# Folded spectra for six batches, a gate spread over two quarters, and a last block finished tile by tile

## The chip, the cores and the metric

The kernel is one program on one core of a Trainium2 chip. TensorE multiplies, VectorE, ScalarE and GpSimd work on vectors, and SyncE issues the DMAs; the five run side by side and meet at semaphores. The metric is the device time of one execution in microseconds; less is better. Three runs of the kernel before took 1412.92 to 1415.26 us.

## The reference

Three layers follow each other. The first is an attention with landmarks, on 8 batches of 8 heads, 576 tokens and 64 features:

```python
A = sm(q, k_lm); Bm = sm(q_lm, k_lm); C = sm(q_lm, k)     # 32 landmarks: means over 18 tokens
Z = Bm.T / (norm1(Bm) * norminf(Bm) + 1e-6)
for _ in range(6): Z = 2 * Z - Z @ Bm @ Z
x = A @ Z @ C @ v                                          # heads side by side: [8, 576, 512]
```

The second mixes tokens and features by a Fourier transform and has a network with 2048 hidden features:

```python
u = x + real(fft(fft(x, axis=1), axis=2))
y = u + relu(layernorm(u) @ w_ch1) @ w_ch2
```

The third is a gated network with 1024 hidden features, on y and on y shifted by one token:

```python
k = relu((mu_k * y + (1 - mu_k) * y_prev) @ w_k)
out = sigmoid((mu_r * y + (1 - mu_r) * y_prev) @ w_r) * (k * k @ w_v)
```

## The kernel before, in words

The work comes in two units. A batch (`phase1`, eight of them, 0 to 7) does the attention and the Fourier transform of its 576 tokens. A block is 512 tokens; there are 9, 0 to 8. Each block goes through the second layer's network (class `Block`) and later through the third layer (class `Gated`).

A planner orders everything. Each operation of each engine is recorded with a cost and with what it depends on; then the planner places the operations one after the other, on each engine the ready one with the highest key. A key is the length of work behind the operation plus a lead, and `LEADS` holds an added lead for each part of a batch or of the weights' conversion. So one list of numbers decides the order on all five engines. TensorE's products of the blocks are a chain in a fixed order; the products of the batches are woven between them. A batch takes a PSUM bank from those that the blocks don't hold.

In a batch, `chain_a` makes the scores A against the landmarks. Tokens s and 576 − s stand beside each other (`A[c][:, 0]` and `[:, 1]`), in three tiles of 96 or 97 rows. Their sums and differences (`Ae`, `Ao`) are rounded to two f16 halves. The spectra over tokens are products of these with a cosine and a sine table of 289 columns: for each of two groups g and each table, three tiles times three pairs of halves (`PARTS`), nine products into one bank. `keep` rounds a spectrum to two f16 halves again, by a ScalarE copy and a VectorE operation. Behind that, `chain_a` transposes A itself (`AT`). `tail` uses spectra and transposes to make the batch's rows of u.

A block of the second layer has four quarters. In blocks 2 to 8 each quarter is made of seven smaller products of sums of operands (`Block.first`); the operands 0 to 6 of a block (`un`) are f16 halves, and in `run(ps, w, b, ...)` the number b names the operand: 0, 4, 5, 6, 3, 2, 1 in this order. Between the seven stand the steps of the quarter before (`second`).

A block of the gated network has two quarters (`Gated.first`, g 0 and 1), n = 2i + g in all. Beside the quarter's seven products of `w_k`, `fillers(n)` puts the steps of the quarter before (`second`) and, in the first quarter of each block, the seven products of the gate (`gate`). The gate's products share one PSUM bank: each adds to, or starts anew in, the bank that ScalarE or VectorE has just read. For n = 0 there is no quarter before. For n = 18 only the last quarter's steps are left, and the last step of each pair of output tiles is followed by a VectorE operation on each tile and a store of 256 KB.

The cosine and sine tables lie in constant memory for the whole first phase.

Of the kernel before, what the change touches and what calls it, by code (L numbers as in the profile page):

```python
# [23 lines left out]
M = 32  # L24
DM = H * D
# [6 lines left out]
HS = S // 2 + 1  # L32
WS = 64.0
# [104 lines left out]
class Op:  # L138
# [14 lines left out]
    ("back", 0): 427,  # L153
    ("back", 1): 2988,
    ("back", 2): -34,
    ("back", 3): -54,
    ("back", 4): 45,
    ("back", 5): -35,
    ("back", 7): -119,
    ("items", 0): 50,  # L160
    ("keys", 0): 61,
    ("keys", 1): -243,
    ("keys", 2): 1030,
    ("keys", 3): 261,
    ("keys", 4): -206,
    ("keys", 5): -130,
    ("keys", 6): -9,
    ("keys", 7): -191,
    ("land", 0): 509,
    ("land", 1): -1287,  # L170
    ("land", 2): -1291,
    ("land", 3): -771,
    ("land", 4): -488,
    ("land", 5): -427,
    ("land", 7): -18,
    ("norm", 0): 29,
    ("norm", 1): 2257,
    ("norm", 2): -59,
    ("norm", 5): 13,
    ("norm", 7): 148,  # L180
    ("own", 0): -2,
    ("own", 1): 169,
    ("own", 3): -3,
    ("own", 5): 809,
    ("own", 6): -23,
    ("own", 7): 51,
    ("prep", 0): 214,
    ("prep", 1): -163,
    ("prep", 2): -253,
    ("queries", 1): 141,  # L190
    ("queries", 2): 16,
    ("queries", 3): 11,
    ("queries", 4): 4,
    ("queries", 5): 57,
    ("queries", 7): -23,
    ("scales", 0): -5,
    ("series", 0): 343,
    ("series", 1): 447,
    ("series", 2): -156,
    ("series", 3): -89,  # L200
    ("series", 4): -108,
    ("series", 5): -66,
    ("series", 6): 1,
    ("series", 7): 63,
    ("sums", 1): 114,
    ("sums", 2): -77,
    ("sums", 3): -392,
    ("w1", 0): 3,
    ("w1", 1): -655,
    ("w1", 2): 258,  # L210
    ("w1", 3): 59,
    ("w2", 0): 8,
    ("w2", 1): -454,
    ("w2", 2): -64,
    ("w2", 3): 149,
# [55 lines left out]
class Plan:  # L271
# [455 lines left out]
def phase1(a, iss, psum, const, pool, ident, ublock, ones):  # L727
# [21 lines left out]
    def load_q(b):  # L749
        q = T["q", b] = tile([128, 4, 2 * HS], "q")  # L750
# [30 lines left out]
    def landmarks(b):  # L781
# [21 lines left out]
        step = 2 if b else 1  # L803
        for h in range(0, 4, step):
            sl = slice(h, h + step)
            for o, c in ((0, 0), (16, 290)):
                v_.tensor_reduce(
                    qs[:, sl, o:o + 16],
                    q[:, sl, c:c + 288].rearrange("p c (g t) -> p c g t", t=18),
                    axis=AX.X, op=ALU.add,  # L810
                )
# [3 lines left out]
    def chain_a(b):  # L815


        q, kbd = T["q", b], T["kbd", b]
        A = [
            tile([128, 512], f"A{c}")[0:97].rearrange("p (x m) -> p x m", x=2) for c in range(3)  # L820
        ]

        if b:

            ST = tile([128, 4 * HS], "ST", "s2").rearrange("p (a g s) -> p a g s", a=2, g=2)
            for ab in range(2):
                ph = psum(2)
                for p in range(4):
                    for g in range(2):
                        r = slice(64 * g, 64 * g + 64)  # L830
                        mm(
                            ph[g][M * p:M * p + M, 0:HS], kbd[r, p, g],
                            q[r, p, HS * ab:HS * ab + HS],
                            True, True, beside=2, tile_position=(64 * g, M * p),
                        )
                for g in range(2):
                    s_.activation(ST[:, ab, g], ph[g][:, 0:HS], AF.Copy)

        def scores(c):
            ps = psum()[0]  # L840
            if b:
                for ab in range(2):
                    for g in range(2):
                        o = 256 * ab + 128 * g
                        tr(ps[0:97, o:o + 128], ST[:, ab, g, 96 * c:96 * c + 97], ident)
            else:
                ps4 = ps.rearrange("p (a g h m) -> p a g h m", a=2, g=2, m=M)
                for ab in range(2):
                    o = HS * ab + 96 * c
                    for p in range(4):  # L850
                        mm(ps4[0:97, ab, :, p], q[:, p, o:o + 97], kbd[:, p], True, True)
            p3 = ps[0:97, :].rearrange("p (g m) -> p g m", m=M)
            mx = tile([97, 16], "mx", bufs=2)
# [3 lines left out]
                e, p3, mx.unsqueeze(2).to_broadcast([97, 16, M]), op=ALU.subtract  # L857
# [3 lines left out]
        def normalize(c):  # L861
            e = A[c].rearrange("p a (h m) -> p (a h) m", m=M)
            sm = tile([97, 16], "sm", bufs=2)
# [4 lines left out]
                e, e, sm.unsqueeze(2).to_broadcast([97, 16, M]), op=ALU.mult  # L868
# [3 lines left out]
        for c in range(3):  # L872
# [4 lines left out]
            iss.tile(pool, [128, 2, 768], F16, n).rearrange("p x (c m) -> p x c m", c=3)[0:97]  # L877
            for n in ("Ae", "Ao")
        ]
        for c in range(3):  # L880
            for x, op, n in ((Ae, ALU.add, "d1"), (Ao, ALU.subtract, "d2")):
                d = tile([128, HS], n)[0:97, 0:256]
# [4 lines left out]
        acs = tile([128, 4 * HS], "acs", "s2")  # L887
# [21 lines left out]
        def keep(dst, g, ps, scale, pair_scale):  # L909
            n = wide(ps)  # L910
            if b < HALF:
                s_.activation(dst[:, g, 0:n], ps, AF.Copy, scale=scale)
                return
            hi, lo = dst[:, 0, g, 0:n], dst[:, 1, g, 0:n]
# [4 lines left out]

        for g in range(2):  # L920
# [1285 lines left out]
```

## Time and profile before

| | |
|---|---|
| time, median of 3 runs | 1413.22 us (1412.92 to 1415.26) |
| the profiled execution | 1416.67 us, its span 1414.9 us |
| TensorE busy, matmuls | 1398.1 us (99%) |
| VectorE busy | 1003.2 us (71%) |
| ScalarE busy | 799.0 us (56%) |
| GpSimd busy | 462.7 us (33%) |
| mean granted clock of TensorE | 0.996 |
| DMA | 213.05 MB, mean 151 GB/s |

Times in the rows below are from the start of the span. A busy TensorE is not TensorE at its peak: matmuls overlap, and the time of one in a group is longer than the distance from its start to the next one's. PE is TensorE, DVE is VectorE, ACT is ScalarE, POOL is GpSimd, and PEld is the weight load that goes before each matmul. In a name such as `gp<-c_cosT,Ae` the output stands left of the arrow and the inputs right of it, without buffer numbers.

### The profile page before, as it was taken

The page shows a single profiled execution, that of the slowest core. Times are in us where ns is not written, and L with a number is a line of the kernel's source. Part 1 is how long each engine was busy: PE and PEld are TensorE (multiplying, and loading weights), DVE is VectorE, ACT ScalarE, POOL GpSimd, SP SyncE. Part 2 cuts the span into 40 slices and gives each one's busy share as a digit, 9 for nine tenths or more (in the row PEclk, how much of TensorE's full clock was granted, in tenths as well). Part 3 has the DMA queues.
Part 4 walks back from the last instruction along what each step waited for, and adds up shares of the span by engine and source line. Part 5 has one row for each costly group of instructions (what it writes and reads, how often), then busy time and mean ns, then how long its engine had stood idle before and what let it go on. Part 6 is the DMA issues. An engine that isn't in the chain of part 4 may idle for free.

```text
span 1414.9 us, 26712 instructions
## 1 busy us (share of the span) xinstructions
PE 1398.1 (99%) x10575; PEld 909.6 (64%) x10575; DVE 1003.2 (71%) x1934; ACT 799.0 (56%) x1579; POOL 462.7 (33%) x546
## 2 busy tenths in 40 slices
PE   8999999999999999999999999999999999999998
PEld 5555454566676666666666666666667767776775
DVE  7988874776886876886867785327778776876532
ACT  4876543454545545545565453226887767867552
POOL 3013254343252251253322270103545533652400
PEclk9999999999999999999999999999999999999999
DMA  9795763673664564654477553423110011010001
GB/s 340 262 343 177 243 240 104 211 265 121 224 205 134 201 225 138 203 186 135 151 238 289 228 194 121 157 110 120 31 61 31 31 61 61 23 38 31 31 1 60
DMA packets 86780, 213.05 MB, mean 151 GB/s; under 512 B 7168, under 2 KB 28416, under 8 KB 80384
## 3 DMA queue, kind: packets, MB, share of 16 engines
q1 hardware_dynamic: 86656, 211.36, 43.2%
q8 instruction: 83, 1.36, 0.4%
q14 instruction: 41, 0.34, 0.1%
HBM read 168.08 MB, written 43.25 MB: 149 GB/s over the span
## 4 chain that ended last, share of the span: by engine, by line
PE 90%; DVE 3%; DMA 3%; POOL 1%; ACT 1%; issue 1%; SPq 0%; DVEq 0%; ACTq 0%
PE acc L420 37%; PE ph L420 33%; PE gp L420 16%; PE gp L437 2%; DVE xt L264 2%; DMA dw<-wboth 1%; PE spare L1371 1%; DMA wst<-in_w_v 1%; DMA v<-in_v 1%; DMA wst<-in_w_ch 1%; POOL xr L264 1%; SPq L405 0%; DVE k L264 0%; POOL tmp L264 0%; DVE rm L264 0%
## 5 line engine op out<-in xcount | busy, mean ns | idle before, releaser
L420 PEld LDWEIGHTS <-w 128*128 128x128 f16 x4464 | 430.2, 98 | 268.5 <-issue 30.4
L420 PE MATMUL acc<-h,w 128*128 128x512 f16 x1728 | 429.4, 379 | 0.0
L420 PE MATMUL ph<-un,w 128*128 128x256 f16 (+1 forms) x2736 | 394.4, 288 | 1.5 <-DVE un L264 1.4
L420 PE MATMUL acc<-w_v,k 128*128 128x512 f16 x864 | 204.3, 379 | 0.0
L264 DVE TENSOR_TENSOR rm<-ph,rm 128x512 f32<-128x512 f32 x138 | 95.0, 688 | 136.4 <-ACT rm L264 97.8
L264 ACT ACTIVATE rm<-ph 128x512 f32<-128x512 f32 x156 | 93.1, 597 | 174.2 <-PE ph L420 173.8
L420 PE MATMUL ph<-xk,w_k 128*128 128x256 f16 x1512 | 180.1, 273 | 0.0
L420 PEld LDWEIGHTS <-w_k 128*128 128x128 f16 x1512 | 147.7, 98 | 27.0
L420 PEld LDWEIGHTS <-k 128*128 128x128 f16 x864 | 84.5, 98 | 78.7
L264 POOL TENSOR_TENSOR xk<-xt,xk 128x512 f16<-128x512 f32 x63 | 89.9, 1440 | 135.0 <-ACT xk L264 131.8
L264 POOL TENSOR_TENSOR xr<-xt,xr 128x512 f16<-128x512 f32 x63 | 90.8, 1455 | 21.5 <-ACT xr L264 21.5
L420 PE MATMUL gp<-w_r,xr 128*128 128x256 f16 x756 | 93.0, 273 | 3.2 <-DVE gm L264 2.1
L264 ACT ACTIVATE rm<-rm 128x512 f32<-128x512 f32 (+1 forms) x134 | 84.3, 630 | 12.6 <-DVE rm L264 9.5
L420 PEld LDWEIGHTS <-xr 128*128 128x128 f16 x756 | 73.9, 98 | 24.3 <-issue 4.0
L264 ACT ACTIVATE h<-rm 128x512 f16<-128x512 f32 x84 | 52.7, 627 | 62.1 <-DVE rm L264 61.6
L264 DVE SCALAR_TENSOR_TENSOR k<-rm,k 128x512 f16<-128x512 f32 x72 | 56.0, 781 | 25.2 <-ACT k L264 25.2
L264 DVE SCALAR_TENSOR_TENSOR h<-rm,h 128x512 f16<-128x512 f32 x84 | 63.3, 757 | 11.6 <-ACT h L264 11.3
L264 DVE TENSOR_TENSOR xt<-xt 128x512 f32<-128x512 f32 x52 | 70.4, 1373 | 1.5 <-POOL xr L264 1.1
L264 POOL TENSOR_TENSOR A<-A,sm 97x512 f32<-97x512 f32 x24 | 27.8, 1157 | 117.7 <-DVE sm L264 93.8
L264 ACT ACTIVATE h<-ph 128x512 f16<-128x512 f32 x60 | 35.7, 595 | 49.9 <-PE ph L420 49.5
L264 DVE SCALAR_TENSOR_TENSOR h<-ph,h 128x512 f16<-128x512 f32 x60 | 41.3, 688 | 28.1 <-ACT h L264 27.9
L264 DVE SCALAR_TENSOR_TENSOR xt<-yb,mus,xt 128x512 f32<-128x512 f32 x72 | 54.7, 809 | 6.9 <-POOL xt L264 6.9
(222 smaller groups left out, 2041.2 us busy)
## 6 DMA issues: line engine op xcount, KB each, us to landing
w<-dw SPq DMA_DIRECT2D x60, 1024.0 KB, 7.2
w<-dwp SPq DMA_DIRECT2D x56, 384.0 KB, 5.7
ys<-ub SPq DMA_DIRECT2D x36, 256.0 KB, 7.4
out<-sg SPq DMA_DIRECT2D x36, 256.0 KB, 2.1
yb<-ys SPq DMA_DIRECT2D x8, 1026.0 KB, 5.3
v<-in_v SPq DMA_DIRECT2D x8, 1024.0 KB, 8.2
wst<-in_w_ch SPq DMA_DIRECT2D x16, 512.0 KB, 6.5
q<-in_q SPq DMA_DIRECT2D x14, 578.0 KB, 4.9
```

Source lines behind the costliest of these rows:

```text
L264: f(real(out), *map(real, args), **{k: real(x) for k, x in kw.items()})
L420: self.nc.tensor.matmul(out.real(), lhsT=lhsT.real(), rhs=rhs.real(), start=start, stop=stop, **kw)
L437: self.nc.tensor.transpose(out.real(), in_.real(), ident.real())
L1371: nc.tensor.matmul(into.real() if into else spare[0], lhsT=z.to_broadcast([128, 128]), rhs=z.to_broadcast([128, 512]), start=not into, sto ...
```

## The change

The spectra of batches 2 to 7 are folded once more. The tokens 0 to 288 are ordered in three runs, `RUNS`: 0 to 90, the odd ones from 91, the even ones from 90. The columns of q are laid out in that order by the host for these batches. The output frequencies s and 288 − s share the sums over even tokens and, up to a sign, the sums over odd tokens. So `folded` makes two sums of 145 columns each, over even and over odd tokens, four groups of three products in all, in one bank. ScalarE copies the odd sums out, VectorE writes sum and difference as one spectrum of 289 columns, and `keep` rounds that as before. The tables `cosP` and `sinP` are new. Batches 0 and 1 keep the old way, and their tables are now one load into a place that the operands 4, 5 and 6 of blocks 2 to 8 use later. The transposes `AT` write their columns of PSUM with a step of two for two of the three runs.

In the gated network the last two products of block 0's gate move from its first to its second quarter. At the end, the last quarter's steps go tile by tile, and the last of the four tiles is multiplied and stored in two halves of columns.

The planner's cost of a transpose depends on its width now, and `LEADS` is another list throughout; three of its lines stand here for all.

```diff
+QS = S // 4 + 1
+RUNS = (range(0, 91), range(91, 288, 2), range(90, 289, 2))
+TS = 290
...
-    ("back", 0): 427,
-    ("back", 1): 2988,
-    ("back", 2): -34,
...
+    ("back", 0): 808,
+    ("back", 1): 3753,
+    ("back", 2): 292,
...
-        self.record("pe", run, 0.108, [out], [in_, ident])
+        self.record("pe", run, wide(ident) / 1200.0 + 0.003, [out], [in_, ident])
...
-    cosT = load_const("cosT", [128, 2, 3, HS], F16)
-    sinT = load_const("sinT", [128, 2, 3, HS], F16)
+    cosT, sinT = [early[:, n] for n in range(2)]
+    iss.load(early, a["early"])
     cs = load_const("cs", [128, 4, 512])
+    iss.lead = 0.0
+    cosP = load_const("cosP", [128, 2, 4, QS], F16)
+    sinP = load_const("sinP", [128, 2, 4, QS], F16)
+    iss.lead = was
...
+        else:
+            for h in range(4):
+                for o, c, n in ((0, 0, 0), (16, TS + 1, 1)):
+                    v_.tensor_reduce(
+                        qs[:, h, o:o + 5], q[:, h, c:c + 90].rearrange("p (g t) -> p g t", t=18),
+                        axis=AX.X, op=ALU.add,
+                    )
+                    c += 91 - 2 * n
+                    v_.tensor_reduce(
+                        qs[:, h, o + 5:o + 16],
+                        q[:, h, c:c + 198 + 2 * n].rearrange("p (x n) -> p x n", x=2)[
+                            :, :, n:99 + n
+                        ].rearrange("p x (g t) -> p g x t", t=9),
+                        axis=AX.XY, op=ALU.add,
+                    )
...
+        RP, AT0, w = (97, (0, 96, 192), HS) if b < HALF else (100, (0, 91, 190), TS)
...
+        def spectrum(g, src, tab, dst):
+
+            ps = psum()[0]
+            for c in range(3):
+                r = 97 if c == 2 else 96
+                for n, (x, y) in enumerate(PARTS):
+                    mm(
+                        ps[:, 0:HS], src[0:r, x, c, 128 * g:128 * g + 128],
+                        tab[0:r, y, c, :], c == 0 and n == 0, c == 2 and n == 2,
+                    )
+            keep(dst, g, ps[:, 0:HS], 1.0 / SA, 1.0 / SC)
+
+        def folded(g, src, tab, dst, sign):
+
+            ps = psum()[0]
+            for x, parts in enumerate((((0, 0), (2, 3)), ((0, 1), (1, 2)))):
+                o = QS * x
+                for k, (c, n) in enumerate(parts):
+                    r = len(RUNS[c])
+                    for m, (i, j) in enumerate(PARTS):
+                        mm(
+                            ps[:, o:o + QS], src[0:r, i, c, 128 * g:128 * g + 128],
+                            tab[0:r, j, n, :], k == 0 and m == 0, k == 1 and m == 2,
+                        )
+            even, odd = ps[:, 0:QS], tile([128, QS], "odd")
+            full = tile([128, HS], "full")
+            s_.activation(odd, ps[:, QS:2 * QS], AF.Copy, scale=1.0 / SA)
+            v_.scalar_tensor_tensor(
+                full[:, 0:QS], even, 1.0 / SA, odd, op0=ALU.mult, op1=ALU.add
+            )
+            v_.scalar_tensor_tensor(
+                full[:, HS - 1:QS - 1:-1], even[:, 0:QS - 1], sign / SA, odd[:, 0:QS - 1],
+                op0=ALU.mult, op1=ALU.subtract if sign > 0 else ALU.add,
+            )
+            keep(dst, g, full, 1.0, SA / SC)
...
+            if b < HALF:
+                spectrum(g, Ae, cosT, AC)
+                spectrum(g, Ao, sinT, AS)
+            else:
+                folded(g, Ae, cosP, AC, 1.0)
+                folded(g, Ao, sinP, AS, -1.0)
...
+        runs = (RUNS[0][:-1], *RUNS[1:])
+        if b < HALF:
+            runs = [range(96 * c, 96 * c + (97 if c == 2 else 96)) for c in range(3)]
         for ab in range(2):
             for g in range(2):
                 ps = psum()[0]
-                n = HS if ab == 0 else 288
-                for c in range(3):
-                    r = 97 if c == 2 and ab == 0 else 96
+                for c, run in enumerate(runs):
+                    n = len(run)
                     tr(
-                        ps[:, 96 * c:96 * c + r], A[c][0:r, ab, 128 * g:128 * g + 128],
-                        ident[0:r, 0:r],
+                        ps[:, run[0]:run[-1] + 1:run.step], A[c][0:n, ab, 128 * g:128 * g + 128],
+                        ident[0:n, 0:n],
                     )
-                keep(AT[ab], g, ps[:, 0:n], 1.0 / SA, 1.0)
+                keep(AT[ab], g, ps[:, 0:HS], 1.0 / SA, 1.0)
...
+        early = iss.place(pa, [128, 2, 2, 3, HS], F16, "early", "more_un")
+        batch = phase1(a, iss, gp, p1c, p1w, ident, ublock, ones, early)
...
+            more = iss.spot(pa, [128, 3, 2, 2, HB], F16, "un", "more_un")
 
             def split(at, t):
-                un[at] = hi, lo = [
+                un[at] = hi, lo = [more[:, at - 4, x] for x in range(2)] if at > 3 else [
                     iss.tile(pa, [128, 2, HB], F16, "un", f"un{x}{at}") for x in "hl"
...
-                if not closes:
-                    return
+                if closes:
+                    self.store(js)
+
+            def last(self, j):
+                iss.lead = NOW
+                sl = slice(128 * j, 128 * j + 128)
+                for f in self.order[4:]:
+                    for n, (x, y) in enumerate(PARTS):
+                        mm(
+                            self.acc[j], self.ks[f // 4][:, x, f % 4, sl],
+                            ws[f"w_v{f // 4}"][:, y, f % 4], False,
+                            f == self.order[-1] and n == 2, chain=True,
+                        )
+                self.store((j,), 2 if j == 3 else 1)
+
+            def store(self, js, parts=1):
+                w = DM // parts
                 for j in js:
                     o = self.sg[j]
-                    v_.scalar_tensor_tensor(
-                        o, self.acc[j], self.qi[:, j:j + 1], self.sg[j],
-                        op0=ALU.mult, op1=ALU.mult,
-                    )
                     r0 = BLK * self.i + 128 * j
-                    iss.load(a["out"][r0:r0 + 128, :], o)
+                    for c in range(0, DM, w):
+                        v_.scalar_tensor_tensor(
+                            o[:, c:c + w], self.acc[j][:, c:c + w], self.qi[:, j:j + 1],
+                            o[:, c:c + w], op0=ALU.mult, op1=ALU.mult,
+                        )
+                        iss.load(a["out"][r0:r0 + 128, c:c + w], o[:, c:c + w])
...
-                return [late]
+                return [[partial(blocks[u].last, j) for j in range(4)]]
             if g:
-                return [late[0:1], late[1:3], late[3:5], late[5:6], late[6:7], late[7:8]]
+                full = [late[0:1], late[1:3], late[3:5], late[5:6], late[6:7], late[7:8]]
+                for k, x in enumerate(held):
+                    full[2 * k].append(x)
+                held.clear()
+                return full
...
+            if n == 0:
+                held.extend(gates[5:])
+                return [[x] for x in gates[:5]]
```

## Rows read from the trace of the kernel before

**Rows 1.** The page: busy time of each engine, share of the span, instructions.

```profile
PE 1398.1 (99%) x10575; PEld 909.6 (64%) x10575; DVE 1003.2 (71%) x1934; ACT 799.0 (56%) x1579; POOL 462.7 (33%) x546
```

**Rows 2.** Busy time of each engine in six stretches, granted clock, DMA share, GB/s.

```profile
0.00:75.00 75.00, 69.81 (x589) 42.93 (x589) 62.69 (x165) 50.57 (x119) 13.57 (x28) 0.93 0.84 293
75.00:850.00 775.00, 770.37 (x6034) 480.71 (x6023) 591.32 (x1306) 405.78 (x860) 272.92 (x339) 1.00 0.59 202
850.00:970.00 120.00, 120.00 (x794) 77.17 (x792) 46.08 (x79) 35.19 (x58) 6.03 (x14) 1.00 0.37 132
970.00:1010.00 40.00, 37.01 (x301) 28.87 (x300) 31.40 (x46) 33.99 (x61) 23.05 (x23) 1.00 0.15 54
1010.00:1395.00 385.00, 384.79 (x2795) 272.07 (x2793) 265.71 (x333) 268.54 (x476) 147.16 (x142) 1.00 0.11 39
1395.00:1414.90 19.90, 16.08 (x83) 7.82 (x81) 6.04 (x9) 4.92 (x8) 0.00 (x0) 1.00 0.15 54
```

**Rows 3.** Timeline of TensorE, two spectra of batch 5: start, length, instruction, count.

```profile
504.51 2.40 PE L420 MATMUL gp<-c_cosT,Ae 96*128 96x289 f16 x18
506.75 0.38 PE L420 MATMUL acc<-h,w 128*128 128x512 f16 x1
```

**Rows 4.** Timeline of TensorE, first quarter of the gated network; brackets: idle before, releaser.

```profile
974.93 0.39 PE L420 MATMUL gp<-eye,r 128*128 128x128 bf16 x4
...
987.09 1.47 PE L420 MATMUL gp<-w_r,xr 128*128 128x256 f16 x12 [0.70 <-ACT sg L264]
...
989.35 1.47 PE L420 MATMUL gp<-w_r,xr 128*128 128x256 f16 x12 [0.78 <-DVE gm L264]
991.95 1.47 PE L420 MATMUL gp<-w_r,xr 128*128 128x256 f16 x12 [1.13 <-DVE gm L264]
993.25 2.78 PE L420 MATMUL ph<-xk,w_k 128*128 128x256 f16 x24
```

**Rows 5.** Groups of instructions by shape, TensorE: busy us, mean ns of one, idle.

```profile
L420 PE MATMUL ph<-xk,w_k 128*128 128x256 f16 x1512 | 180.1, 273 | 0.0
L420 PEld LDWEIGHTS <-w_k 128*128 128x128 f16 x1512 | 147.7, 98 | 27.0
...
L437 PE MATMUL gp<-ident,A 96*128 96x96 f32 x80 | 10.7, 246 | 0.0
...
L420 PE MATMUL gp<-eye,r 128*128 128x128 bf16 x36 | 4.1, 219 | 0.0
```

**Rows 6.** The same view, roundings of the spectra on VectorE and ScalarE.

```profile
L264 DVE SCALAR_TENSOR_TENSOR acs<-gp,acs 128x289 f16<-128x289 f32 x24 | 10.3, 454 | 15.8 <-ACT acs L264 15.8
...
L264 ACT ACTIVATE acs<-gp 128x289 f16<-128x289 f32 x24 | 9.2, 412 | 22.5 <-PE gp L420 22.4
```

**Rows 7.** Timelines of VectorE and TensorE where block 7 is made ready.

```profile
773.85 1.28 DVE L264 SCALAR_TENSOR_TENSOR uc<-uc,gp 128x512 f32<-128x512 f32 x2
...
780.96 2.78 PE L420 MATMUL ph<-un,w 128*128 128x256 f16 x24
```

**Rows 8.** Timeline of TensorE, third product of a last quarter, next block's first two.

```profile
870.71 1.47 PE L420 MATMUL ph<-un,w 128*128 128x256 f16 x12
...
882.42 2.78 PE L420 MATMUL ph<-un,w 128*128 128x256 f16 x24
```

**Rows 9.** The first table's instructions: count, ns, first and last start in us.

```profile
L420 PE MATMUL gp<-c_cosT,Ae x144: 284/287/290, 34.2 to 715.6; 96*128 96x289 f16 x96, 97*128 97x289 f16 x48
L405 SPq DMA_DIRECT2D c_cosT<-in_cosT x1: 328/328/328, 10.7 to 10.7; - x1
```

**Rows 10.** Timeline of the end, and the page's row of the output stores.

```profile
1397.96 13.11 PE L420 MATMUL acc<-w_v,k 128*128 128x512 f16 x60
...
1400.87 0.69 DVE L264 SCALAR_TENSOR_TENSOR k<-rm,k 128x512 f16<-128x512 f32 x1 [1.42 <-ACT k L264]
1409.17 2.73 DVE L264 SCALAR_TENSOR_TENSOR sg<-acc,qi,sg 128x512 f32<-128x512 f32 x4 [7.60 <-PE acc L420]
...
out<-sg SPq DMA_DIRECT2D x36, 256.0 KB, 2.1
```

More of the change, by code (lines that the diff above doesn't have):

```diff
@@ L174 @@
[L174 to L215, printed above, removed]
+    ("back", 0): 808,
+    ("back", 1): 3753,
@@ new lines @@
+    ("back", 2): 292,
+    ("back", 3): 2,
+    ("back", 4): 804,
+    ("back", 5): 255,
+    ("back", 6): 170,
+    ("back", 7): 349,
+    ("keys", 1): -347,
+    ("keys", 2): 842,
+    ("keys", 3): -200,
+    ("keys", 4): -24,
+    ("keys", 5): -20,
+    ("keys", 6): 10,
+    ("keys", 7): 107,
+    ("land", 0): -297,
+    ("land", 1): -653,
+    ("land", 2): -89,
+    ("land", 3): -333,
+    ("land", 4): -544,
+    ("land", 5): -74,
+    ("land", 6): -180,
+    ("land", 7): -185,
+    ("norm", 0): 138,
@@ new lines @@
+    ("norm", 1): 3084,
+    ("norm", 3): -30,
+    ("norm", 4): 102,
+    ("norm", 6): 511,
+    ("norm", 7): -99,
+    ("norm", 8): -30,
+    ("own", 1): 500,
+    ("own", 2): 23,
+    ("own", 3): -84,
+    ("own", 4): 146,
+    ("own", 5): 150,
+    ("own", 6): -6,
+    ("own", 7): 404,
+    ("pairs", 0): -315,
+    ("prep", 1): 70,
+    ("prep", 2): 140,
+    ("queries", 1): 90,
+    ("queries", 2): 148,
+    ("queries", 3): 85,
+    ("queries", 4): -18,
+    ("queries", 5): 301,
+    ("queries", 6): 622,
@@ L216 @@
+    ("queries", 7): 11,
+    ("series", 1): 1044,
+    ("series", 2): -102,
+    ("series", 3): -103,
+    ("series", 4): -41,
+    ("series", 5): -137,
+    ("series", 6): -95,
+    ("sums", 0): 7,
+    ("sums", 1): -85,
+    ("sums", 2): 30,
+    ("sums", 3): 448,
+    ("w1", 1): -468,
+    ("w1", 2): 34,
+    ("w1", 3): 376,
+    ("w2", 0): 5,
+    ("w2", 1): -312,
+    ("w2", 3): 246,
 }
@@ L749, in load_q @@
     def load_q(b):
-        q = T["q", b] = tile([128, 4, 2 * HS], "q")
+        q = T["q", b] = tile([128, 4, 2 * TS], "q")
         step = 2 if b else 1
@@ L802, in landmarks @@
         qs = tile([128, 4, M], "qs")
[L803 to L810, printed above, removed]
-                )
+        if b < HALF:
+            step = 2 if b else 1
+            for h in range(0, 4, step):
+                sl = slice(h, h + step)
+                for o, c in ((0, 0), (16, 290)):
+                    v_.tensor_reduce(
+                        qs[:, sl, o:o + 16],
+                        q[:, sl, c:c + 288].rearrange("p c (g t) -> p c g t", t=18),
+                        axis=AX.X, op=ALU.add,
[5 more added lines that the diff above has]
+                        qs[:, h, o:o + 5], q[:, h, c:c + 90].rearrange("p (g t) -> p g t", t=18),
+                        axis=AX.X, op=ALU.add,
+                    )
+                    c += 91 - 2 * n
+                    v_.tensor_reduce(
+                        qs[:, h, o + 5:o + 16],
[4 more added lines that the diff above has]
+                    )
         qbd = T["qbd", b] = tile([128, 4, 2, M], "qbd")
@@ L886, in chain_a @@
         at = tile([128, 1280], "at", "s1")
-        acs = tile([128, 4 * HS], "acs", "s2")
+        acs = tile([128, 4 * TS], "acs", "s2")
         def halves(x):
@@ L2144, in consts @@
             sinT[r, c] = np.sin(ang) if s not in (0, 288) else 0.0
+    cosP = np.zeros((128, 4, QS))
+    sinP = np.zeros((128, 4, QS))
+    sp = np.arange(QS)
+    for c, run in enumerate((RUNS[0][:-1], *RUNS[1:])):
+        for r, s in enumerate(run):
+            ang = 2 * np.pi * ((s * sp) % S) / S
+            w = 0.5 if s in (0, 288) else 1.0
+            n = s % 2 if c == 0 else c + 1 if c == 1 else 3
+            cosP[r, n] = w * np.cos(ang)
+            sinP[r, n] = np.sin(ang) if s not in (0, 288) else 0.0
     cs = np.zeros((128, 4, 512))
@@ L2161, in layout @@
     qa = q[:, HPOS].reshape(B, 2, 4, S, D).transpose(0, 2, 1, 4, 3).reshape(B, 4, 128, S)
-    cols = list(range(HS)) + [0] + [S - j for j in range(1, HS)]
-    qh = np.ascontiguousarray(qa[..., cols])
+    fold = [s for run in RUNS for s in run]
+    cols = np.array([
+        [*range(HS), 0, *(S - j for j in range(1, HS)), 0, 0],
+        [*fold, *((S - s) % S for s in fold)],
+    ])[[0] * HALF + [1] * (B - HALF)]
+    qh = np.ascontiguousarray(np.take_along_axis(qa, cols[:, None, None, :], axis=-1))
     kh = np.ascontiguousarray(
```

76 lines of the change are left out of this document (24 added, 52 removed).

## The prediction

> **What bounds the kernel now.** I read the busy row of the page first: TensorE is busy 99% of the span, and no other engine is above 71% [rows 1]. A busy TensorE can still be a waiting one, so the stretches come next. From 75 to 850 us, where batches 2 to 7 are woven into the blocks of the first network, TensorE is without work for 4.6 of 775 us; from 850 to 970 us for nothing; from 1010 to 1395 us for 0.2. Three stretches leave it idle: the start (75 − 69.8 = 5.2 us), the passage into the gated network from 970 to 1010 us (3.0 us) and the end (3.8 us) [rows 2]. VectorE is at 591 of 775 us in the long stretch and ScalarE at 406. So three rules follow. Work taken off TensorE between 75 and 970 us shortens the run one for one, as long as the rest keeps up. Work put on VectorE or ScalarE there costs nothing while it is not late. A wait counts only in the three stretches named. The timelines then give the prices.
>
> **Part 1, folded spectra (batches 2 to 7).** Removed: 4 spectra of 9 products over 289 columns in each of 6 batches. In the timeline 18 of them begin at 504.51 and the next work at 506.75 us, so one takes 2.24 / 18 = 124 ns [rows 3]; 36 x 124 ns = 4.48 us a batch, 26.9 us in all. Added: 4 spectra of 12 products over 145 columns, 48 a batch. The trace of before has no full-width product of 145 columns, so I put it between neighbours. Four products of 128 columns, each with its own 128 x 128 weights, take 0.39 us from first start to last end, and one lasts 219 ns: (390 − 219) / 3 = 57 ns [rows 4, 5]. Twenty-four of 256 columns take 2.78 us, one lasts 273 ns: (2780 − 273) / 23 = 109 ns [rows 4, 5]. That is 0.41 ns a column, so 145 columns cost 57 + 17 x 0.41 = 64 ns; 48 x 64 ns = 3.07 us a batch, 18.4 us in all. The difference is 26.9 − 18.4 = 8.5 us, all of it inside the stretch in which TensorE has no slack.
>
> The bound on the other side is the weight load. A load of 128 f16 columns is shown with 98 ns [rows 5]. If loads could not overlap each other, 48 pairs would take 4.70 us against 4.48 and part 1 would cost 0.2 us a batch. I take 64 ns, because the four pairs at 57 ns each carry such a load and are the nearest row in width.
>
> Here a rule speaks against the change. The Trainium skill, page "TensorE: Matmul & The Clock Gate", section "Back-to-back issue gap", says that a stream of weight load and product pairs sustains about 81 ns at 128 columns and 131 ns at 512. By these, as an estimate, 145 columns would cost 83 ns and 289 columns 102 ns, and part 1 would add 0.3 us a batch instead of taking 1.4. The trace disagrees at both widths that it shows, 57 ns at 128 and 124 ns at 289 [rows 3 to 5], so I go by the trace.
>
> Each folded spectrum also adds a ScalarE copy of 145 columns and two VectorE operations of 145 and 144. For 289 columns these engines need 412 and 454 ns [rows 6], so at most 0.41 + 2 x 0.45 = 1.3 us a spectrum, 5.2 us a batch, and at least half of that, since the width is halved. VectorE takes on at most 24 x 0.9 = 22 us beside its 591 of 775, ScalarE 10 beside 406. The sixteen shorter sums over the queries in place of four make VectorE's share a little larger still. The cover is TensorE's own chain of blocks, which fills every gap while a batch is at VectorE. What is late next is the batch: batch 7's normalization writes its last operand source at 773.85 + 1.28 = 775.1 us, and the buffer it wants next is released by the first 12 products that start at 780.96, at 782.3 us [rows 7]. So 7.1 us of lateness are free, against at most 5.2. Cost zero.
>
> The transposes behind the spectra now write every second column of PSUM, eight of twelve a batch. No row shows such a write. One of them is shown with 10.7 / 80 = 134 ns at most [rows 5]; none extra if stride is free, and 8 x 6 x 134 ns = 6.4 us if it doubles them. I take zero, since the columns per transpose, 90 to 100 for 96 and 97, are the same, and keep 6.4 for the range.
>
> The old tables and three of the seven operand pairs now share a place. Operand 4 of the next block can no longer be written when its own buffer is free but only after the third product of the last quarter, which starts at 870.71 and ends near 872.0; it is first needed by the second product from 882.42, at 883.7 [rows 8]. Splitting it takes one operation on ScalarE and one on VectorE, so 11.7 us hold some 1.5. Cost zero. The first user of the place, block 2, comes after batch 1 is through with the tables.
>
> At the start the two tables come as one load of twice the size. The first of them was issued at 10.7 us and first used at 34.2 [rows 9], so 23 us stand for what is now one load. The folded tables, 0.6 MB more, are issued at a lower priority. Cost zero.
>
> **Part 2, gate over two quarters.** In the first quarter of the gated network nothing is left over to put between the gate's seven products, which all use one PSUM bank and so wait for its eviction. The waits stand at 987.09 (0.70 us), 989.35 (0.78) and 991.95 us (1.13) [rows 4]. The sixth and seventh product move into the second quarter, each behind products of the next stage. Those two waits, 1.9 us, go. The fifth product's wait of 0.70 stays: its release, the sigmoid, is not moved. TensorE then comes to the second quarter 1.9 + 2.6 us sooner, and what it asks for there, squares of the first quarter, must be ready. The half that is made last is wanted after 60 products of 256 columns and 24 of 512, by 0.109 us [rows 4] and 13.11 / 60 = 0.22 us [rows 10] each some 11.8 us, so I count no new wait. Gain 1.9 us; nothing if the eviction chain only makes the next product wait instead.
>
> **Part 3, the end.** Tile by tile, the last tile's products end when the last products ended before: 60 products stay 60 [rows 10]. Their inputs are wanted earlier: after 12 + 6 products of 0.22 us from 1397.96, at 1401.9 us, and they are ready at 1400.87 + 0.69 = 1401.6. That is close but no wait. Behind the last product stood one VectorE operation, 2.73 / 4 = 0.68 us, and a store that takes 2.1 us to land [rows 10]. Two halves need between 0.68 and 1.36 us, and the last store is half as large, so it may save up to 1.05 us or cost 0.68; halves overlap in part, and I take zero.
>
> **Sum.** −8.5 − 1.9 + 0 = −10.4 us. The profiled execution took 1416.67 us, of which the span is 1414.9; it becomes 1406.3, with a span of 1404.5. The median of the runs shown is 1413.22, 3.4 below it; the same subtraction gives **1402.8 us**, 0.7% faster. A difference under 0.2%, 2.8 us, is no change here.
>
> The list of priorities is new too, so every engine's order changes. What it can win is the idle time left, 4.6 us up to 850 and part of 5.2 at the start [rows 2], where the granted clock is 0.93 on average; what it can lose I set equal, 5 us.
>
> **Rivals.**
> The weights bind: 145-column products cost a weight load's 98 ns. Then part 1 costs 1.3 us, part 2 gives 1.9, and the time is 1412.6, no change. For it: the page's rule above. Against it: 57 ns pairs. Chance 0.05.
>
> The order loses what the columns gave: 3 to 8 us of new idle time, or strided transposes at 6.4: 1406 to 1411. For it: the start waits on loads and evictions, and any new order moves them. Chance 0.15.
>
> The order wins: idle time of 4 to 7 us goes as well: 1396 to 1399. For it: the idle exists; against it, it is in pieces. Chance 0.13.
>
> The batches come late (the other side): a spectrum is now a chain of product, copy, two combinations and the old pair of roundings, with one buffer each for the odd half and the whole. If a batch is late by more than the 7.1 us above, TensorE's chain of blocks stops at each of six block starts. It decides beyond 7.1 + (10.4 + 2.8) / 6 = 9.3 us; with twice my 5.2, 10.4 us, it is 6 x 3.3 − 10.4 = +9.4, and 1422.6 us. Against it: that takes twice the upper bound. Chance 0.06.
>
> No effect, because the batches already hide in time that something else sets: speaks against it that TensorE has no idle time there. 1413. Chance 0.03.
>
> **How the numbers follow.** The forecast with its own range, 1399 to 1406, has 0.58. Faster by over 0.2%: 0.58 + 0.13 + most of 0.15 = 0.84. Same: 0.05 + 0.03 and the rest, 0.09. Slower: 0.06 and a little more, 0.07. The range for 8 in 10 runs from the order that wins to the order that loses, 1396 to 1411.
>
> **What would show it.** Products of 145 columns start 64 ns apart, 288 of them (98 would refute part 1). TensorE's idle time from 75 us to the last block stays under 6 us. The second half of the gate shows no wait on its eviction. The last store starts about as long after the last product as before. Wrong it would be through waits before a block's first products, or a start that ends later than before.

## The result and the profile after

The changed kernel takes 1403.51 us (median of 6 runs, 1401.71 to 1403.63) beside 1415.16 us for the kernel before (median of 6, 1412.92 to 1415.3): ratio 0.9918, interval 0.9905 to 0.9931, 11.7 us less. The forecast was 10.4 us less and 1402.8 us. The profiled execution took 1403.63 us with a span of 1401.8. The span before was 1414.9, so the two traces differ by 13.1 us, more than the medians: the profiled execution before, 1416.67 us, was longer than each of the six runs beside it. The six runs of the changed kernel lie at 1401.7 and at 1403.5 us, with mean granted clocks of 0.998 and of 0.997 to 0.998, and what parts the two groups is not shown.

The stretches of the changed kernel, cut where its own stages end: busy time of each engine, granted clock, DMA share, GB/s.

```profile
0.00:75.00 75.00, 70.24 (x558) 41.34 (x559) 61.91 (x165) 50.22 (x118) 13.50 (x28) 0.95 0.85 298
75.00:850.00 775.00, 773.10 (x6209) 486.36 (x6203) 591.72 (x1412) 398.47 (x860) 255.93 (x317) 1.00 0.58 200
850.00:960.00 110.00, 110.00 (x728) 70.59 (x727) 66.52 (x96) 52.25 (x87) 26.37 (x38) 1.00 0.46 165
960.00:1000.00 40.00, 38.32 (x309) 29.57 (x307) 30.95 (x48) 33.75 (x61) 21.51 (x20) 1.00 0.13 46
1000.00:1382.00 382.00, 382.00 (x2781) 270.74 (x2780) 261.47 (x330) 268.23 (x474) 139.00 (x144) 1.00 0.11 40
1382.00:1401.80 19.80, 15.51 (x78) 7.45 (x76) 6.43 (x10) 4.38 (x7) 0.00 (x0) 1.00 0.15 54
```

Read beside [rows 2], TensorE is without work for 1.9 us instead of 4.6 from 75 to 850 us, and for 1.7 instead of 3.0 in the passage to the gated network; start and end change little (4.8 and 4.3 us, 5.2 and 3.8 before). VectorE is at 592 of 775 us in the long stretch, the same as before; over the whole run it grew from 1003.2 [rows 1] to 1019.0 us.

Folded products in the timeline of TensorE, one spectrum of batch 2:

```profile
201.13 0.93 PE L423 MATMUL gp<-c_sinP,Ao 91*128 91x145 f16 x12
201.90 0.60 PE L423 MATMUL acc<-h,w 128*128 128x512 f16 x2
```

Twelve of 145 columns take 0.77 us to the next work, 64 ns each, against 124 [rows 3]; one is shown with 226 ns, and (930 − 226) / 11 is 64 as well.

The passage to the gated network, the same view (brackets: idle before, releaser):

```profile
959.41 2.78 PE L423 MATMUL ph<-xk,w_k 128*128 128x256 f16 x24
...
968.00 1.47 PE L423 MATMUL gp<-w_r,xr 128*128 128x256 f16 x12 [0.34 <-ACT gm L267]
...
976.12 1.47 PE L423 MATMUL gp<-w_r,xr 128*128 128x256 f16 x12 [1.34 <-ACT sg L267]
977.43 2.78 PE L423 MATMUL ph<-xk,w_k 128*128 128x256 f16 x24
...
981.35 1.47 PE L423 MATMUL gp<-w_r,xr 128*128 128x256 f16 x12
```

The first quarter now ends with the fifth gate product at 976.12, and the second quarter begins at 977.43. The waits of 0.78 and 1.13 us ahead of the sixth and seventh product [rows 4] are gone; the sixth and the seventh run in the second quarter, at 981.35 and 990.46, with no wait. The fifth product's wait has grown from 0.70 to 1.34 us.

The end, TensorE and VectorE, and the landing of the last stores:

```profile
1384.39 13.11 PE L423 MATMUL acc<-w_v,k 128*128 128x512 f16 x60
...
1387.30 0.69 DVE L267 SCALAR_TENSOR_TENSOR k<-rm,k 128x512 f16<-128x512 f32 x1 [1.42 <-ACT k L267]
...
1394.95 0.75 DVE L267 SCALAR_TENSOR_TENSOR sg<-acc,qi,sg 128x512 f32<-128x512 f32 x1 [1.84 <-PE acc L423]
1397.55 0.88 DVE L267 SCALAR_TENSOR_TENSOR sg<-acc,qi,sg 128x256 f32<-128x256 f32 x2 [1.84 <-PE acc L423]
```

```profile
DMA to landing us min/median/max: 1.7/2.0/2.2
```

As in [rows 10], 60 products close the run, in 13.11 us. Each tile but the last is evicted while the next is multiplied. The inputs made last are ready at 1387.99, before their use. A store of half the size lands after 1.7 us instead of 2.0.

Five marks of the two traces divide the 13.1 us. The first product of block 0 starts at 66.7 us (66.2 before), +0.5. From there to the first product of the gated network it takes 892.7 us (904.8), −12.1; no_fold below, with the products of the kernel before in the same order up to there, takes 904.2, so 0.6 us of this differ between executions. The first quarter takes 18.0 us, 20.6 with the two products that left it (22.2), −1.6. From the second quarter to the last 60 products it takes 407.0 us, 404.3 without the two that came (404.7), −0.4. From there to the end of the span it takes 17.4 us (16.9), +0.5.

### The profile page after: what moved, and what is told of

It reads as the page before. It is cut to its first block, busy times and chain, and to the rows that moved or that the text cites. A ratio compares the mean times of both kernels' runs of the same rounds, so it can differ in the third digit from the quotient of the medians.

```text
span 1401.8 us, 26994 instructions
## 1 busy us (share of the span) xinstructions
PE 1389.2 (99%) x10648; PEld 906.1 (65%) x10648; DVE 1019.0 (73%) x2055; ACT 807.3 (58%) x1603; POOL 456.3 (33%) x546
## 4 chain that ended last, share of the span: by engine, by line
PE 97%; DVE 1%; ACT 1%; issue 0%; POOL 0%; DVEq 0%; ACTq 0%; POOLq 0%
PE acc L423 40%; PE ph L423 36%; PE gp L423 18%; PE gp L440 3%; PE spare L1429 1%; DVE xt L267 1%; DVE bdY L267 0%; ACT Y L267 0%; DVE uc L267 0%; DVE ub L267 0%; ACT rm L267 0%; POOL Ae L267 0%; ACT L267 0%; ACT Ae L267 0%; ACT xk L267 0%
## 5 line engine op out<-in xcount | busy, mean ns | idle before, releaser
L267 POOL TENSOR_TENSOR xr<-xt,xr 128x512 f16<-128x512 f32 x63 | 84.2, 1358 | 91.2 <-DVE gm L267 50.6
L267 POOL TENSOR_TENSOR xk<-xt,xk 128x512 f16<-128x512 f32 x63 | 86.9, 1397 | 60.6 <-ACT xk L267 60.1
L267 DVE SCALAR_TENSOR_TENSOR xt<-yb,mus,xt 128x512 f32<-128x512 f32 x72 | 60.9, 882 | 23.0 <-POOL xt L267 21.7
L267 DVE SCALAR_TENSOR_TENSOR k<-rm,k 128x512 f16<-128x512 f32 x72 | 58.0, 810 | 22.9 <-ACT k L267 22.8
L267 DVE TENSOR_TENSOR xt<-xt 128x512 f32<-128x512 f32 x52 | 64.3, 1244 | 6.9 <-POOL xk L267 4.2
L267 POOL TENSOR_TENSOR A<-A,sm 100x512 f32<-100x512 f32 (+1 forms) x24 | 26.9, 1122 | 93.4 <-DVE sm L267 79.9
L267 POOL TENSOR_TENSOR sq<-sq 128x512 f32<-128x512 f32 x18 | 23.9, 1327 | 96.1 <-ACT sq L267 96.1
```

What stands on the lines that cost most here:

```text
L267: f(real(out), *map(real, args), **{k: real(x) for k, x in kw.items()})
```

## The experiments

Each changes the changed kernel or the kernel before in one place. Ratios are to the kernel before, run on the same chip beside it; the changed kernel's own is 0.9918 (0.9905 to 0.9931).

| run | median us | ratio, interval |
|---|---|---|
| wide | 1409.96 | 0.9962 (0.9948 to 0.9975) |
| no_gate | 1407.19 | 0.9939 (0.9927 to 0.9952) |
| no_last | 1402.12 | 0.9907 (0.9892 to 0.9921) |
| old_leads | 1409.07 | 0.9952 (0.9938 to 0.9967) |
| no_fold | 1414.02 | 0.9990 (0.9981 to 0.9999) |
| new_leads | 1436.18 | 1.0152 (1.0138 to 1.0166) |
| combine_twice | 1410.38 | 0.9974 (0.9965 to 0.9983) |
| held_three | 1403.24 | 0.9917 (0.9904 to 0.9931) |
| old_list_no_zeros | 1411.47 | 0.9978 (0.9969 to 0.9986) |
| new_list_no_zeros | 1434.05 | 1.0144 (1.0127 to 1.0161) |
| combine_planned | 1404.87 | 0.9930 (0.9918 to 0.9941) |
| shaken_a | 1418.68 | 1.0030 (1.0019 to 1.0041) |

### Are the columns what counts?

**wide.** The table is padded and read past its part; the planner is told 145 columns, so the order stays.

```diff
-                            ps[:, o:o + QS], src[0:r, i, c, 128 * g:128 * g + 128],
-                            tab[0:r, j, n, :], k == 0 and m == 0, k == 1 and m == 2,
+                            ps[:, o:o + 218], src[0:r, i, c, 128 * g:128 * g + 128],
+                            tab[0:r, at:at + 218], k == 0 and m == 0, k == 1 and m == 2,
+                            planned=QS,
```

> The changed kernel in the same order on every engine, but each of the 288 folded products has 218 columns instead of 145 (the 73 more are never used). Theory A, the columns set the time: 288 x 73 columns at 0.41 ns are 8.7 us more than the changed kernel, 1412.2 us, and no new idle time of TensorE. Theory B, the gain comes from the new order and the columns are hidden: at most 2 us more. Theory C, a product costs at least its weight load's 98 ns: 218 columns cost 93 ns by columns and 98 by the load, the same price as before, so nothing is added.

```profile
L425 PE MATMUL gp<-c_cosP,Ae x144: 254/256/260, 195.2 to 720.8; 91*128 91x218 f16 x72, 100*128 100x218 f16 x36, 99*128 99x218 f16 x36
```

```profile
75.00:850.00 775.00, 773.01 (x6145) 489.20 (x6134) 586.84 (x1403) 393.06 (x853) 256.09 (x317) 1.00 0.58 199
```

The ratio rises by 0.0044, 6.2 us. The two profiled executions, which start block 0 at 66.6 and 66.7 us, differ by 1410.1 − 1401.8 = 8.3 us, close to theory A's 8.7. TensorE is without work for 2.0 us from 75 to 850 us, as in the changed kernel (1.9). Both traces have the same products in the same order. Compared start by start, 7.9 of the 8.5 us that this one loses up to the gated network lie between one folded product and the next. Theories B and C fall: the columns are not hidden, and 145 columns do not already cost a weight load's 98 ns.

**no_fold.** The kernel before with the new `fillers`, `last` and `store`.

```diff
+            if n == 0:
+                held.extend(gates[5:])
+                return [[x] for x in gates[:5]]
...
-                return [late]
+                return [[partial(blocks[u].last, j) for j in range(4)]]
```

> The kernel before with only the gate over two quarters and the last block tile by tile; spectra, tables and priorities as before. Theory A, the columns made most of the gain: 1.5 to 2.5 us faster than before, ratio 0.9985. Theory B: the spectra were hidden, so the gain is the gate's and the end's and the order's; also about 2 us, but then the list alone must bring 9 us.

It is 0.0010 faster than before, 1.4 us (0.1 to 2.7), a little under theory A's range. So parts 2 and 3 without part 1 bring about a tenth of the gain. Theory B expects nearly the same time here; what speaks against it is that the list alone does not bring 9 us (new_leads below). In the trace, the way from the gated network's first product to that of its second block takes 39.5 us, against 41.8 in the kernel before.

### The gate and the end

**no_gate.**

```diff
-            if n == 0:
-                held.extend(gates[5:])
-                return [[x] for x in gates[:5]]
```

> The changed kernel with all seven products of block 0's gate back in its first quarter. Theory A: the two waits come back, 1.6 to 1.9 us slower than the changed kernel, 1405.3 us. Rival, the waits were only handed on: within 0.5 us of the changed kernel.

TensorE's timeline, the fifth to the seventh product of the gate:

```profile
976.42 1.47 PE L423 MATMUL gp<-w_r,xr 128*128 128x256 f16 x12 [1.33 <-ACT sg L267]
978.87 1.47 PE L423 MATMUL gp<-w_r,xr 128*128 128x256 f16 x12 [0.98 <-DVE gm L267]
981.27 1.47 PE L423 MATMUL gp<-w_r,xr 128*128 128x256 f16 x12 [0.94 <-DVE gm L267]
```

The ratio rises by 0.0021, 3.0 us. Two waits of 0.98 and 0.94 us are back, and between the same marks the passage takes 22.9 us against 20.6, 2.2 us more. About 1.0 us more is lost in the later blocks (399.0 us from gated block 1's first product to the last product, 397.9 in the changed kernel), and what loses it is not shown. The waits had not been handed on.

**held_three.**

```diff
-                held.extend(gates[5:])
-                return [[x] for x in gates[:5]]
+                held.extend(gates[4:])
+                return [[x] for x in gates[:4]]
```

> The changed kernel with three products of block 0's gate in the second quarter instead of two. Theory A: the wait of 1.34 us for the sigmoids ahead of the fifth product is hidden by other products too, 1.0 to 1.3 us faster than the changed kernel, 1402.3 us. Rival, TensorE comes to the next stage before its operands are ready: no gain.

```profile
1022.81 1.47 PE L423 MATMUL gp<-w_r,xr 128*128 128x256 f16 x12 [0.45 <-DVE gm L267]
...
1025.94 1.47 PE L423 MATMUL gp<-w_r,xr 128*128 128x256 f16 x12 [0.36 <-DVE gm L267]
```

The 1.34 us ahead of the fifth product are gone, and without the product that left it the first quarter is 1.6 us shorter. But the time is that of the changed kernel, and its span too (1401.9). From gated block 1's first product to the last product it takes 399.2 us instead of 397.9, so most of the 1.6 us is lost again there. Two waits of that block's gate on VectorE, 0.45 and 0.36 us, are new and make 0.8 of it. The rival holds: TensorE came too early for what VectorE was preparing.

**no_last.**

```diff
-                return [[partial(blocks[u].last, j) for j in range(4)]]
+                return [late]
```

> The changed kernel with the last quarter's steps in the old order and four whole stores at the end. Theory A: the last product and the last store's length set the end in both, so within 0.5 us of the changed kernel, 1403.5 us. Rival, tile by tile was worth its halves: 1 us slower.

The intervals overlap; part 3 is worth nothing that can be measured here. From the last product's end to the end of the span it is 3.9 us, in the changed kernel 4.3; but the kernels with whole stores show 3.8 to 4.2 (before, new_leads) and those with halves 3.8 to 4.3 (old_leads, the changed kernel), so the difference isn't the halves'. The last store lands 2.7 us after the last product with halves and 3.0 with whole stores; the span ends 1.5 and 0.9 us after that, with something else.

### The time at VectorE and ScalarE

**combine_twice.** The three new operations of each spectrum are issued twice inside one planned operation, so every engine's order stays.

```diff
+            iss.times = 2
             s_.activation(odd, ps[:, QS:2 * QS], AF.Copy, scale=1.0 / SA)
...
+            iss.times = 1
             keep(dst, g, full, 1.0, SA / SC)
```

> The changed kernel in the same order on every engine, with the copy and the two combinations of each folded spectrum executed twice (the second time they write the same values): 24 more ScalarE and 48 more VectorE operations in the way of the batches. Theory A, the batches have some 7 us to spare at VectorE and ScalarE: within 1 us of the changed kernel. Rival, the longer chain of a batch is already at its limit: 24 spectra x 1 us, up to 24 us slower.

It is 0.0056 slower than the changed kernel, 7.9 us; the spans differ by 8.7. I had expected nothing. What TensorE waited for, and its busy time from 200 to 850 us:

```profile
PE gp L427 <- DVE RX L270: 2.6, 7, 0.5
PE gp L444 <- DVE full L270: 2.2, 6, 0.5
```

```profile
200.00:850.00 650.00, 643.83 (x5262) 414.33 (x5261) 493.20 (x1194) 320.55 (x702) 215.44 (x269) 1.00 0.55 189
```

One such wait, with the product of a block that comes next:

```profile
397.41 0.44 PE L444 MATMUL gp<-ident,A 90*128 90x90 f32 x3 [0.29 <-DVE full L270]
397.69 1.03 PE L427 MATMUL acc<-h,w 128*128 128x512 f16 x4
```

The waits stand at products of the batches, most of them transposes and products of the series (`RX`): TensorE stops there for 0.2 to 0.5 us, in most places with products of a block right behind. The order on TensorE is fixed, and it doesn't take them first. The transposes read only A, so what they wait for at `full` is the PSUM bank that the combination has to read first. TensorE's idle time from 75 to 850 us grows by 4.8 us only, less than the loss, since a wait is counted from a product's shown end: a product of 512 columns is shown with 379 ns, while the next one starts 216 ns behind it. Compared start by start with the changed kernel, whose products stand in the same order, nearly all of the 8.5 us lost up to the gated network lie at such places. Theory A falls, and the rival's limit of 24 us is not reached: added operations of 0.9 us a spectrum (0.29 + 0.31 + 0.30 below) cost 8 / 24 = 0.33 us each.

**combine_planned.** The same operations, but recorded twice.

```diff
+            for _ in range(2):
+                s_.activation(odd, ps[:, QS:2 * QS], AF.Copy, scale=1.0 / SA)
...
```

> The changed kernel with the copy and the two combinations of each folded spectrum recorded twice, so that the planner knows of the second ones and orders around them. Theory F, the 8 us that unplanned ones cost come from a fixed order that holds TensorE at the next product of the batch, and a planned delay is covered by the blocks: within 3 us of the changed kernel, 1406.5 us at most. Rival G, a batch has no time to spare however it is ordered: 8 us slower again, 1411 us.

```profile
200.00:850.00 650.00, 648.43 (x5311) 419.12 (x5310) 498.98 (x1209) 329.35 (x719) 212.86 (x271) 1.00 0.56 193
```

Told of them, the planner lets blocks' products pass first: 1.4 to 1.7 us slower than the changed kernel instead of 8, with intervals that overlap, and TensorE is busy for 648.4 of 650 us again (648.6 in the changed kernel). Theory F holds: a batch does have time to spare, but only where the order has been written with it.

### What the list of priorities is worth

**old_leads** is the changed kernel with the old `LEADS`, **new_leads** the kernel before with the new one.

```diff
 LEADS = {
-    ("back", 0): 808,
-    ("back", 1): 3753,
...
+    ("back", 0): 427,
+    ("back", 1): 2988,
...
```

> The changed kernel with the old list of priorities; only the order changes. Theory A: what the list is worth is idle time of TensorE, 1 to 4 us slower than the changed kernel, up to 1407.5 us. Theory B: the list made the gain, so 8 us slower or more, 1411 us and above.

> The kernel before with only the new list of priorities. Theory A: the list was chosen for other work; within 3 us of before on either side, 1412 to 1418 us. Theory B, the order made the gain: 8 us faster or more, 1407 us and below.

With the old list the changed kernel is 0.0034 slower, 4.8 us, a little more than theory A's 1 to 4. It keeps more than half of its gain, which speaks against theory B. The new list makes the kernel before 0.0152 slower, 21.5 us: both theories missed that. In both traces something new stands on TensorE, products with zeros into the blocks' accumulators (old_leads first, then new_leads):

```profile
L1429 PE MATMUL acc<-zero x26: 377/381/390, 281.8 to 497.6; 128*128 128x512 f16 x26
```

```profile
L1371 PE MATMUL acc<-zero x51: 378/380/390, 118.6 to 799.3; 128*128 128x512 f16 x51
```

The planner puts them where its plan leaves TensorE idle inside a block's accumulation; the changed kernel and the kernel before have none. TensorE is busy with them for 6.9 and 13.4 us (the expectations below say 7.5 and 14.5), so I asked whether they are the loss.

**old_list_no_zeros** and **new_list_no_zeros** leave them out.

```diff
-            if op.opens is not None:
-                warming.append(op.opens)
```

> The changed kernel with the old list of priorities, without the products with zeros that the planner puts where its plan leaves TensorE idle between the blocks' first and last accumulation (26 of them with that list, 7.5 us in the trace). Theory D, these products stand where the chip has work, so they are TensorE's time: 5 to 7 us faster than with them, 1402 to 1404 us, and the old list would be as good as the new one. Rival E, the idle time in which they stand is real: within 1.5 us of the time with them, 1409 us, and TensorE idle for 7 us more.

> The kernel before with the new list of priorities, without the products with zeros (51 of them, 14.5 us in the trace). Theory D: 12 to 14.5 us faster than with them, 1421 to 1424 us. Rival E, the plan's idle time is real: within 2 us of the time with them, 1434 us and above.

They are not. Without them the one is 0.0026 slower, the other no faster than its interval. For the first, 250 to 500 us with and without them (columns as above):

```profile
250.00:500.00 250.00, 248.47 (x2059) 159.96 (x2056) 197.27 (x468) 122.68 (x269) 92.83 (x116) 1.00 0.56 189
```

```profile
250.00:500.00 250.00, 244.48 (x2031) 158.30 (x2030) 198.12 (x468) 122.05 (x269) 92.11 (x116) 0.99 0.55 187
```

TensorE is then idle where they had been, 5.5 us instead of 1.5, and the granted clock falls for a part of it. For the second, 75 to 200 us:

```profile
75.00:200.00 125.00, 121.48 (x892) 64.06 (x881) 102.99 (x232) 77.44 (x170) 38.48 (x45) 1.00 0.63 226
```

```profile
75.00:200.00 125.00, 116.34 (x798) 61.72 (x794) 102.28 (x232) 76.29 (x170) 38.47 (x45) 0.97 0.64 224
```

Idle grows from 3.5 to 8.7 us and the clock is 0.97. Theory D falls: a list that doesn't fit the kernel makes real idle time, and the products with zeros stand in it. Theory E holds for the second. The first is 3.7 us slower where E allowed 1.5, and its trace does not show all of that: the profiled execution is the shortest of the twelve, with a mean granted clock of 0.997. In the other eleven it is 0.992 to 0.995, with the products with zeros 0.996 to 1.000. So taking them out also went with a lower clock here.

**shaken_a.**

```diff
+LEADS = {k: v + 60 * (-1) ** n for n, (k, v) in enumerate(LEADS.items())}
```

> The changed kernel with its list of priorities shaken: 60 added to every second lead and taken from the others. It sizes what a list alone is worth on the changed kernel. Theory A, the list is worth a few us of idle time: 1 to 5 us slower than the changed kernel, 1404.5 to 1408.5 us. Rival: the list doesn't matter, within 0.5 us.

It is 0.0112 slower than the changed kernel, 15.8 us, more than either theory allowed. The stretches of the shaken kernel and, behind it, the changed one:

```profile
67.00:75.00 8.00, 7.10 (x58) 3.44 (x58) 7.29 (x19) 6.50 (x16) 0.00 (x0) 0.84 0.97 368
75.00:200.00 125.00, 119.66 (x828) 62.45 (x827) 100.74 (x239) 75.89 (x165) 25.46 (x31) 0.97 0.69 232
200.00:850.00 650.00, 648.66 (x5302) 418.61 (x5300) 481.19 (x1162) 325.68 (x695) 226.53 (x284) 1.00 0.58 194
```

```profile
67.00:75.00 8.00, 6.65 (x67) 3.07 (x66) 7.83 (x20) 6.97 (x14) 0.00 (x0) 1.00 0.45 135
75.00:200.00 125.00, 124.46 (x891) 65.38 (x885) 105.74 (x257) 79.30 (x174) 40.43 (x48) 1.00 0.71 253
200.00:850.00 650.00, 648.63 (x5319) 420.99 (x5318) 485.99 (x1157) 319.17 (x687) 215.50 (x269) 1.00 0.55 190
```

All of it is lost before block 1. Block 0's first product comes at 71.9 us instead of 66.7, and block 1's at 190.6 instead of 174.9; TensorE lacks work for 5.3 us from 75 to 200 us instead of 0.5, and its clock is 0.84 and 0.97. From 200 to 850 us the two are alike, 648.7 and 648.6. From block 1's first product to the end the shaken kernel even needs 2.5 us less.

## Why the prediction was right, point by point

**Bound.** TensorE's work set the time: wide adds columns in the same order and pays for them in time. Shown.

**Part 1, columns.** 64 ns a product was forecast between the widths of [rows 4, 5], and the timeline shows 64. 216 x 124 − 288 x 64 ns = 8.4 us, as the sum had it (8.5). Of the 12.1 us between the marks, 3.7 are left over. Idle time from 75 to 850 us fell by 2.7 of these. The last 1.0 lies behind products of the blocks and of the series, of which there are as many as before: from start to start they stand closer by 0.35 (`ph<-un,w`), 0.33 (`acc<-h,w`) and 0.32 us (`gp<-RX,bdR`) in all. So these 3.7 us are the order's, or in part the 0.6 by which executions differ, and the forecast had no term for them but its 5 us either way.

**Part 1, covered work.** VectorE and ScalarE need less a spectrum than the bound of 1.3 us:

```profile
L267 DVE SCALAR_TENSOR_TENSOR full<-gp,odd 128x145 f32<-128x145 f32 x24 | 7.3, 306 | 7.8 <-ACT odd L267 7.7
...
L267 DVE SCALAR_TENSOR_TENSOR full<-gp,odd 128x144 f32<-128x144 f32 x24 | 7.1, 297 | 0.0
...
L267 ACT ACTIVATE odd<-gp 128x145 f32<-128x145 f32 x24 | 7.0, 292 | 31.1 <-PE gp L423 31.1
```

Cost zero came true, but the reason given was wrong. It was reckoned from the 7.1 us that block 7's start had to spare, as if any lateness up to there were free. combine_twice shows that it isn't: 8 us lost from some 0.9 us a spectrum, with no new wait at a block's start. What covers such operations is that the planner has their cost when it writes the order (combine_planned).

**Transposes.** Three of them, two with a step of two in PSUM, are shown as one row with 0.42 us; one lasts 246 to 250 ns, so (0.42 − 0.25) / 2 = 85 ns. In the kernel before, with a step of one, it is (0.41 − 0.25) / 2 = 80 ns by the second row. The 6.4 us kept for the range were for a step that doubles the time, and were not needed: here it adds about 5 ns, with 90 to 100 columns for 96.

```profile
397.09 0.42 PE L440 MATMUL gp<-ident,A 90*128 90x90 f32 x3
```

```profile
417.63 0.41 PE L437 MATMUL gp<-ident,A 96*128 96x96 f32 x3
```

**Part 2.** Forecast 1.9 us; 1.6 between the marks, 1.9 of waits and 2.2 in the passage when undone (3.0 by the ratio). Two waits went as foreseen. That the fifth product's wait would stay at 0.70 was off by 0.6 us, and removing it too brings nothing (held_three): what is won here is lost again in the next block, in part on VectorE.

**Part 3.** Forecast zero, and no_last gives no difference.

**The order.** This term was mis-sized most. The prediction gave a new list of priorities 5 us either way. The change came out 1.3 us better than the sum, so it did no harm here; but a shake of 60 costs 15.8 us, and the same list on the kernel before 21.5. That the result was within the range rests on a new list that fits the new kernel. Nothing in the trace of before could tell that, so for this term the forecast was lucky. The chances put on the losing side, 0.15 for an order that loses 3 to 8 us and 0.06 for late batches, were small for what such a list can do.

**Rivals.** Weights that bind: refuted by the 64 ns at 145 columns. The 81 ns at 128 columns of the Trainium skill, page "TensorE: Matmul & The Clock Gate", section "Back-to-back issue gap", don't hold in this kernel, whose rows give 57 ns [rows 4, 5]. No effect: refuted by wide. Batches late: not in the changed kernel, though combine_twice shows its mechanism at a far smaller lateness than the 9.3 us worked out for it, and at the batches' own products rather than at block starts.

## What to carry to other kernels

Where one engine has no slack, count its instructions by a start-to-start distance taken from the neighbouring widths; the sum for the products came out within 0.1 us here, and padding the same instructions without changing the order tests it. Work "hidden" on other engines is only hidden if the fixed order was written with it: 24 times 0.9 us that the planner didn't know of cost 8 us, and 1.4 to 1.7 us once it did. With a list of priorities that fits one program, undoing a part of a change or carrying the list to another program measures the list as well, so keep the order where you can and look at which stretch lost.

## What the runs showed of the hardware

TensorE's granted clock falls towards the end of the start in some executions and stays up in others. The changed kernel's profile and that of no_last, whose order is the same up to the last products:

```profile
50.00:60.00 10.00, 10.00 (x52) 6.98 (x51) 9.03 (x20) 9.25 (x18) 0.00 (x0) 0.90 0.67 236
60.00:70.00 10.00, 8.56 (x49) 4.15 (x50) 8.45 (x26) 7.06 (x17) 0.00 (x0) 0.76 0.88 321
```

```profile
50.00:60.00 10.00, 10.00 (x68) 6.40 (x69) 9.69 (x25) 9.26 (x19) 0.00 (x0) 1.00 0.67 227
60.00:70.00 10.00, 7.90 (x53) 3.65 (x38) 9.61 (x26) 7.79 (x19) 0.00 (x0) 1.00 0.84 317
```

In the first the clock is at 0.90 and 0.76 on average, so at its lower level of 1.2 GHz for some of the time; in the second it stays at 2.4 GHz, and block 0's first product starts at 64.9 instead of 66.7 us. Closer, in the first:

```profile
56.00:58.00 2.00, 2.00 (x20) 2.00 (x20) 2.00 (x5) 1.75 (x4) 0.00 (x0) 1.00 1.05 442
58.00:60.00 2.00, 2.00 (x12) 2.00 (x12) 1.03 (x3) 1.89 (x6) 0.00 (x0) 0.50 0.92 360
```

In both, TensorE is then in a run of 32 products of one column, which starts at 55.5 and 55.3 us. In the first the clock falls inside this run, and the run takes 4.6 us; in the second it takes 3.6. Whether the clock falls differs from one execution to the next of the same program: the mean granted clock of no_last's four runs is 1.000, 1.000, 0.998 and 0.997. Why it falls in one and not in another is not shown.
